# Joining two partial sums at the end of a decode kernel: fp32 identity products in PSUM, or a move to SBUF and one VectorE add

**Chip, cores, metric.** One core of one Trainium2 chip (trn2). The time is the device time of the kernel in microseconds (us); the kernel before took 367.31 us (median of 3 runs, 366.95 to 367.37). "Faster" or "slower" means a difference of more than 2%.

## The reference, cut to what matters

The output is a gated mix of two branches for 8 batch rows and 576 columns:

```python
a = softmax(q k^T * Dh**-0.5) v @ wo      # 32 heads, a window of 2048 keys, wo: (4096, 576)
b = gelu(layernorm(x) @ w1 + b1) @ w2 + b2  # w2: (4608, 576)
return g * a + (1 - g) * b
```

The kernel folds g and 1 - g into the operands, so that all products with `wo`, with `w2` and with the bias row add up in one accumulator of 8 x 576 fp32 numbers. Only the end of this accumulation is changed.

## The kernel before

The accumulator lies in one PSUM bank. The 576 columns are split into two halves of `JN` = 288 (`NJ` = 2). Each half has two copies, so that four products can run side by side in four column tiles of TensorE (in the trace before, four matmuls start within 0.01 us at 355.07): the first column-tile pair holds the halves at partitions 0 and 32, the second pair holds the same halves at partitions 64 and 96. Groups with `split=2` alternate between the pairs; groups with `split=1` use the first pair alone.

```python
class AccGroup:
    def __init__(self, name, mms, deps, cost, after=(), prio=0, split=2):
        ...
        def fn(e):
            for i, (lhsT, rhs) in enumerate(grp.mms):
                for j in range(NJ):
                    c = 64 * (i % split) + 32 * j
                    ins = e.matmul(ps[c:c + 8, BK_ACC, 0:JN], lhsT, rhs[:, JN * j:JN * j + JN], start=False, stop=True,
                                   skip_group_check=True, tile_position=(0, c))
```

The last chunk of `w2` (9 rows of 576 per partition) comes in three transfers of 4, 4 and 1 rows and goes to the first pair alone. While its first piece is multiplied, ScalarE moves the second pair's sum to SBUF; two fp32 products with an identity (the join) then add it to the first pair; the other pieces follow; at the end VectorE and ScalarE each copy one half to SBUF as bf16.

```python
cuts = [0, 4, 8, 9] if ci == FC - 1 else [0, FJ]
for n, (j0, j1) in enumerate(zip(cuts, cuts[1:])):
    ...                                    # one transfer and one AccGroup for rows j0..j1
    if ci == FC - 1 and n == 0:
        odd = [g_.op for g_ in acc_groups if g_.split == 2]
        o_ac = add("act", lambda e: e.activation(out=accs[64:128, :], in_=ps[64:128, BK_ACC, 0:JN], func=ACTF.Copy), ...)   # L807

        def join_fn(e):
            for j in range(NJ):
                c = 64 + 32 * j
                ins = e.matmul(ps[32 * j:32 * j + 8, BK_ACC, 0:JN], i32[c:c + 32, 0:8], accs[c:c + 32, :], start=False, stop=True,
                               skip_group_check=True, tile_position=(c, 32 * j))                                         # L813
        o_m2.append(add("pe", join_fn, deps=[o_ac], name="join", cost=0.7, after=o_m2[-1:]))
...
for j, (eng, ev) in enumerate((("sp", "dve"), ("act", "act"))):
    ...   # VectorE copies half 0 (L841), ScalarE half 1 (L842); then one output transfer each
```

Of the kernel before, what the change touches and what calls it, by code (L numbers as in the profile page):

```python
# [8 lines left out]
ACTF = mybir.ActivationFunctionType  # L9
ALU = mybir.AluOpType  # L10
# [28 lines left out]
class _Plan:  # L39
# [10 lines left out]
    def add(self, eng, fn, deps=(), name=None, cost=0.1, after=(), prio=0):  # L50
        op = _Op(eng, fn, deps, name, cost, after=after, prio=prio)
        op.idx = len(self.all)
        self.all.append(op)
        return op

    def dma(self, eng, fn, semkey, nbytes, deps=(), name=None, after=(), prio=0):
        op = _Op(eng, fn, deps, name, self.DMA_ISSUE, after=after, is_dma=True, dma_sem=semkey, nbytes=nbytes, prio=prio)
        op.idx = len(self.all)
        self.all.append(op)
        return op  # L60
# [121 lines left out]
def build_kernel(nc, A_x, A_k_cache, A_v_cache, A_wq, A_wo, B_x, B_w1, B_b1, B_w2, B_b2, gate_w, out):  # L182
# [10 lines left out]
    NG = Hkv // HG  # L193
# [6 lines left out]
    NJ = 2  # L200
    WO_CH = 8
    JN = D // NJ
    BIG = 1.0e9
    x2 = A_x.rearrange("b s d -> (b s) d")
    out2 = out.rearrange("b s d -> (b s) d")

    with ExitStack() as es:
# [74 lines left out]
        def view(name, parts=128):  # L282
            o, n, dt = R[name]
            a = arena[0:parts, o // 2: o // 2 + (n * (2 if dt == BF else 4)) // 2]
            if dt == F32:
                a = a.bitcast(F32)
            return a
# [5 lines left out]
        i32 = view("i32")  # L293
# [24 lines left out]
        out_sb = view("out_sb")  # L318
        accs = view("accs")
# [10 lines left out]
        def slot(s):  # L330
            return RAW[:, s * SE:(s + 1) * SE]
# [12 lines left out]
        ps = es.enter_context(nc.psum_tensor("ps", [128, 8, 512], F32))  # L344
# [5 lines left out]
        BK_ACC = 7  # L350
# [7 lines left out]
        add, dma = P.add, P.dma  # L358
# [38 lines left out]
        for s in range(2):  # L397
            o_xz.append(add("dve", (lambda s=s: lambda e: e.tensor_copy(xz[:, s, :].rearrange("p (k z) -> p k z", z=2)[:, :, s], x_sb[:, 512:576]))(),  # L398
                            deps=dx + [o_xz0], name="xz%d" % s, cost=0.12))
# [12 lines left out]
        for s in range(2):  # L412
            o_yz.append(add("dve", (lambda s=s: lambda e: e.tensor_copy(yz[:, s, :].rearrange("p (k z) -> p k z", z=2)[:, :, s], y_bf[:, 512:576]))(),
                            deps=[o_y, o_yz0], name="yz%d" % s, cost=0.12))
# [30 lines left out]
        def b1ev_fn(e):  # L445
# [5 lines left out]
                   deps=[o_dga, o_dgb, o_onesf], name="g_pe", cost=0.4, after=[o_yTp])  # L451
# [9 lines left out]
                    deps=[o_i20, o_ident], name="i2_%d" % q, cost=0.15, prio=-1) for q in range(4)]  # L461
        for q in range(4):
            o_i32.append(add("dve", (lambda q=q: lambda e: e.tensor_copy(i32[32 * q:32 * q + 32, :], ident[32 * q:32 * q + 32, 32 * q:32 * q + 32]))(),
                             deps=[o_ident, o_obl], name="i32_%d" % q, cost=0.15, prio=-1))
# [77 lines left out]
        acc_groups = []  # L542
# [32 lines left out]
        last_dma = [d_w1r]  # L575
# [4 lines left out]
        exp_done, pm_done, pt_done, pv_last = {}, {}, {}, {}  # L580
# [7 lines left out]
        def take_slot():  # L588
            n = n_slot[0]
            n_slot[0] += 1  # L590
            return 4 + n % 5
# [188 lines left out]
                        ds.append(d)  # L780
                AccGroup("proj%d" % c, mms, place_done[c] + ds, cost=1.1)

        o_m2 = []

        def bias(i):
            d = dma("sp", lambda e: e.dma_start(b2_sb, B_b2.partition_broadcast(8)), "b2", 65536, name="d_b2", after=last_dma[-1:])
# [3 lines left out]
        def m2_chunk(ci):  # L790
            s = take_slot()
            dst = slot(s)[:, 0:FJ * D]
            src = B_w2[FCW * ci:FCW * ci + FCW, :].rearrange("(p j) n -> p (j n)", j=FJ)
            cuts = [0, 4, 8, 9] if ci == FC - 1 else [0, FJ]
            ops = []
            for n, (j0, j1) in enumerate(zip(cuts, cuts[1:])):
                def w2_fn(e, j0=j0, j1=j1):
                    return e.dma_start(dst[:, j0 * D:j1 * D], src[:, j0 * D:j1 * D])
                d = dma("sp", w2_fn,
                        ("t%d" % n) if ci == FC - 1 else ("s%d" % s), 128 * (j1 - j0) * D * 2, deps=slot_free[s] if n == 0 else [], name="d_w2_%d_%d" % (ci, n), after=last_dma[-1:])  # L800
                last_dma.append(d)
                mms = [(hT[:, FJ * ci + j, :], dst[:, j * D:(j + 1) * D]) for j in range(j0, j1)]
                ops.append(AccGroup("m2_%d_%d" % (ci, n), mms, [o_hT, d], cost=0.16 * (j1 - j0), after=o_m2[-1:], split=1 if ci == FC - 1 else 2).op)
                o_m2.append(ops[-1])
                if ci == FC - 1 and n == 0:
                    odd = [g_.op for g_ in acc_groups if g_.split == 2]
                    o_ac = add("act", lambda e: e.activation(out=accs[64:128, :], in_=ps[64:128, BK_ACC, 0:JN], func=ACTF.Copy), deps=odd + pt_done[NG - 1], name="acc_ev", cost=0.5, prio=9)  # L807

                    def join_fn(e):
                        ins = None  # L810
                        for j in range(NJ):
                            c = 64 + 32 * j
                            ins = e.matmul(ps[32 * j:32 * j + 8, BK_ACC, 0:JN], i32[c:c + 32, 0:8], accs[c:c + 32, :], start=False, stop=True,  # L813
                                           skip_group_check=True, tile_position=(c, 32 * j))
                        return ins
                    o_m2.append(add("pe", join_fn, deps=[o_ac], name="join", cost=0.7, after=o_m2[-1:]))
                    ops.append(o_m2[-1])
            slot_free[s] = ops

        pv_hist = []  # L820
# [1 line left out]
        for kind, i in stream:  # L822
            if kind == "B":
                project()
            {"K": k_unit, "V": v_unit, "W": wo_chunk, "M": m2_chunk, "B": bias}[kind](i)
            while True:
                if waiting and (waiting[0] < 2 or waiting[0] - 2 in pv_last):
                    softmax(waiting[0])
                    spread(waiting.pop(0))
                elif v_here and v_here[0][0] // 4 in pt_done:  # L830
                    v_compute(*v_here.pop(0))
                else:
                    break

        acc_ops = [g_.op for g_ in acc_groups] + o_m2[-4:]
        fin = []
        for j, (eng, ev) in enumerate((("sp", "dve"), ("act", "act"))):
            def ev_fn(e, j=j, ev=ev):
                dst, src = out_sb[32 * j:32 * j + 8, :], ps[32 * j:32 * j + 8, BK_ACC, 0:JN]
                if ev == "dve":  # L840
                    return e.tensor_copy(dst, src)  # L841
                return e.activation(out=dst, in_=src, func=ACTF.Copy)  # L842
            o_fin = add(ev, ev_fn, deps=acc_ops, name="fin%d" % j, cost=0.4, prio=9)
            fin.append(dma(eng, (lambda j=j: lambda e: e.dma_start(out2[:, JN * j:JN * j + JN], out_sb[32 * j:32 * j + 8, :]))(), "out" if j == 0 else "outb", 8 * JN * 2, deps=[o_fin], name="d_out%d" % j, after=last_dma[-1:]))
        add("sp", lambda e: None, deps=fin, name="final_wait", cost=0.05)

        P.schedule()
# [16 lines left out]
def bass_gated_mix__sliding_block_cached__mixer_channel_mlp__decode_kernel(  # L864
    nc: bass.Bass,
    A_x: bass.AP,
    A_k_cache: bass.AP,
    A_v_cache: bass.AP,
    A_wq: bass.AP,
    A_wo: bass.AP,  # L870
    B_x: bass.AP,
    B_w1: bass.AP,
    B_b1: bass.AP,
    B_w2: bass.AP,
    B_b2: bass.AP,
    gate_w: bass.AP,
    out: bass.AP,
):
    build_kernel(nc, A_x, A_k_cache, A_v_cache, A_wq, A_wo, B_x, B_w1, B_b1, B_w2, B_b2, gate_w, out)
# [28 lines left out]
```

## Time and profile before

| | kernel before |
|---|---|
| time, median of 3 | 367.31 us |
| span of the profiled run | 365.8 us |
| busy: TensorE / VectorE / ScalarE | 66% / 62% / 6% |
| bytes read from HBM, mean rate | 154.31 MB, 422 GB/s |
| second piece of the last w2 chunk landed | 361.91 us |
| first of the ten matmuls behind the join | 362.84 us |
| from that landing to the end of the span | 3.89 us |

The transfer engines are full until the last slice, so only the few microseconds after the last transfers can move. I therefore read every trace by the last two rows: the time from the landing of the second piece to the end of the span does not depend on how late the 154 MB stream happens to end. The landing is the issue plus its time to landing. The lines of the profile stand in the prediction. In them PE is TensorE, PEld its weight loads, DVE VectorE, ACT ScalarE, POOL GpSimd and SP SyncE; SPq and ACTq issue transfers; L555 is line 555 of the kernel. The granted clock is the share of its full speed that TensorE was given, 1.00 or 0.50; I call the latter half clock. In before, each step between the two values comes 3.41 us, or a whole multiple of that, after the step before it (the last four are at 349.75, 353.17, 356.58 and 363.41); hence the stretches of 3.41 us below.

### The profile page before, as it was taken

The numbers are of one execution on the slowest core, as the hardware profiler recorded it, in microseconds if no ns is written. First come the engines' busy times: TensorE is split into PE (matmuls) and PEld (weight loads), VectorE is DVE, ScalarE is ACT, GpSimd is POOL, SyncE is SP. The second block draws the span as 40 slices with busy tenths as digits, with TensorE's granted clock in tenths as the row PEclk, the third lists the DMA queues.
The fourth block names the chain that finished last, engine by engine and source line by source line (L and its number), as shares of the span: only waits on it lengthen the run. The fifth ranks groups of instructions, "written<-read, shape, count | busy, mean of one in ns | idle before, by whom it ended". The sixth has DMA issues, their size and how long they took to land.

```text
span 365.8 us, 3987 instructions
## 1 busy us (share of the span) xinstructions
PE 241.1 (66%) x1683; PEld 114.5 (31%) x1683; DVE 226.3 (62%) x340; ACT 22.7 (6%) x54; POOL 17.4 (5%) x80
## 2 busy tenths in 40 slices
PE   0269684847598749365849294829948398396676
PEld 0259331312253314122514132304414133143332
DVE  4700986576999090869963453699590839975212
ACT  1010000000010000001100000001000000010000
POOL 4021000001000000010000000000000000000000
PEclk9999999689699959696987769787969588768986
DMA  9999999999999999999999999999999999999994
GB/s 393 440 415 421 423 435 443 417 456 401 457 408 447 416 439 437 423 455 407 459 403 457 405 453 408 449 416 446 417 441 423 441 409 442 423 430 432 427 420 170
DMA packets 9546, 154.58 MB, mean 423 GB/s; under 512 B 1036, under 2 KB 1204, under 8 KB 2744
## 3 DMA queue, kind: packets, MB, share of 16 engines
q1 hardware_dynamic: 9472, 154.29, 98.5%
q8 instruction: 13, 0.21, 0.2%
q10 hardware_dynamic: 56, 0.03, 0.0%
q14 instruction: 5, 0.04, 0.0%
HBM read 154.31 MB, written 0.01 MB: 422 GB/s over the span
## 4 chain that ended last, share of the span: by engine, by line
DMA 60%; DVE 25%; PE 12%; issue 2%; SPq 0%; ACT 0%; DVEq 0%
DMA arena<-in_A_k_cache_dram 54%; DVE arena L666 18%; DMA arena<-in_A_v_cache_dram 6%; PE ps L678 6%; PE ps L711 4%; DVE arena L639 3%; PE ps L555 1%; DVE arena L597 1%; DVE arena L761 1%; DVE arena L631 1%; DVE arena L600 0%; DVE arena L606 0%; PE ps L728 0%; PE ps L813 0%; PE ps L612 0%
## 5 line engine op out<-in xcount | busy, mean ns | idle before, releaser
L666 DVE STREAM_TRANSPOSE arena<-arena 128x4096 f32<-128x4096 f32 x32 | 140.7, 4424 | 88.3 <-DMA arena<-in_A_k_cache_dram 87.0
L678 PE MATMUL ps<-arena 128*32 128x512 bf16 x512 | 141.7, 440 | 62.1 <-DVE arena L666 62.1
L678 PEld LDWEIGHTS ps<-arena 128*32 128x32 bf16 x512 | 52.3, 106 | 144.3 <-DVE arena L666 67.2
L711 PE MATMUL ps<-arena 128*32 128x512 bf16 x512 | 60.7, 448 | 24.6 <-DVE arena L602 18.8
L711 PEld LDWEIGHTS ps<-arena 128*32 128x32 bf16 x512 | 24.5, 108 | 51.1 <-issue 31.4
L639 DVE STREAM_TRANSPOSE arena<-arena 128x512 bf16<-128x512 bf16 x32 | 30.8, 1021 | 0.0
L728 PE MATMUL ps<-arena 128*128 128x16 f32 x128 | 17.0, 264 | 5.8 <-ACT arena L722 3.9
L761 DVE COPY arena<-arena 32x4 bf16<-32x4 bf16 (+1 forms) x80 | 12.9, 161 | 11.3 <-POOL arena L749 9.2
L722 ACT ACTIVATE arena<-ps 128x512 f32<-128x512 f32 x16 | 9.6, 597 | 156.6 <-PE ps L711 156.6
L728 PEld LDWEIGHTS ps<-arena 128*128 128x128 f32 x128 | 15.5, 191 | 11.7 <-ACT arena L722 9.6
L749 POOL TENSOR_TENSOR arena<-arena 128x8 bf16<-128x8 f32 x30 | 5.8, 229 | 232.4 <-ACT arena L738 206.9
L510 PE MATMUL ps<-arena 128*128 128x8 bf16 x144 | 10.9, 201 | 2.8 <-DMA arena<-in_B_w_dram 2.8
L510 PEld LDWEIGHTS ps<-arena 128*128 128x128 bf16 x144 | 10.8, 168 | 3.3 <-DMA arena<-in_B_w_dram 3.3
L555 PE MATMUL ps<-arena 128*8 128x288 bf16 (+1 forms) x140 | 10.2, 369 | 2.4 <-DVE arena L761 2.2
L608 ACT ACTIVATE arena<-ps,arena 128x512 bf16<-128x512 f32 x8 | 5.5, 687 | 100.2 <-DVE arena L606 100.2
L597 DVE TENSOR_REDUCE arena<-ps 128x1 f32<-128x512 f32 x8 | 5.5, 691 | 8.8 <-PE ps L678 8.7
L659 POOL TENSOR_TENSOR arena<-arena 128x32 bf16<-128x32 bf16 x32 | 6.4, 239 | 83.7 <-PE ps L678 74.6
L612 PE MATMUL ps<-arena 128*128 128x32 f32 x16 | 3.6, 306 | 8.6 <-DVE arena L611 8.6
L631 DVE TENSOR_SCALAR arena<-arena 128x512 bf16<-128x512 bf16 x32 | 9.0, 323 | 0.0
L425 PE MATMUL ps<-arena 8*128 8x8 bf16 x8 | 0.6, 172 | 10.7 <-DVE arena L398 6.8
L512 PE MATMUL ps<-arena 128*128 128x8 bf16 x36 | 7.2, 201 | 0.0
L555 PEld LDWEIGHTS ps<-arena 128*8 128x8 bf16 (+1 forms) x140 | 4.4, 100 | 8.3 <-DVE arena L761 3.4
(87 smaller groups left out, 79.5 us busy)
## 6 DMA issues: line engine op xcount, KB each, us to landing
arena<-in_A_k_cache_dram SPq DMA_DIRECT2D x16, 4096.0 KB, 25.1
arena<-in_A_v_cache_dram SPq DMA_DIRECT2D x32, 2048.0 KB, 24.3
arena<-in_B_w_dram SPq DMA_DIRECT2D x1, 4608.0 KB, 23.8
arena<-in_A_wo_dram SPq DMA_DIRECT2D x4, 1152.0 KB, 10.0
arena<-in_A_wq_dram SPq DMA_DIRECT2D x1, 4096.0 KB, 13.1
arena<-in_B_w_dram SPq DMA_DIRECT2D x3, 1296.0 KB, 18.0
arena<-in_B_w_dram SPq DMA_DIRECT2D x3, 576.0 KB, 14.6
arena<-in_A_wq_dram SPq DMA_DIRECT2D x1, 512.0 KB, 3.4
```

What stands on the lines that cost most here:

```text
L510: ins = e.matmul(out_, lhsT, yT[:, kt, :], start=(kt == 0), stop=False)
L512: ins = e.matmul(out_, lhsT, yT[:, 4 + c // 2, :], start=False, stop=True)
L555: ins = e.matmul(ps[c:c + 8, BK_ACC, 0:JN], lhsT, rhs[:, JN * j:JN * j + JN], start=False, stop=True, skip_group_check=True, tile_position ...
L597: mx = add("dve", lambda e: e.tensor_reduce(out=k(MX), in_=ps[:, bank, :], axis=AXL.X, op=ALU.max), deps=[qk_done[g]], name="mx%d" % g, co ...
L631: return e.tensor_scalar(out=dst, in0=view("Pd").rearrange("p (s n) -> p s n", s=2), scalar1=amask[:, a:a + 1], scalar2=None, op0=ALU.mult)
L639: return e.transpose(dst, src)
L666: tr = add("dve", (lambda h=h, kb=kb: lambda e: e.transpose(bass.AP(arena_f, offset=foffs("KT") + kb * SE // 2, ap=[[AST // 2, 128], [4, 1 ...
L678: mm = e.matmul(ps[32 * c:32 * c + 32, 2 * (G % 2) + nb, :], qb[:, G % 2, n, 2 * h + ee, :], rhs, start=(h == 0 and t == 0), stop=(h == 1 ...
L711: mm = e.matmul(ps[c:c + 32, bk, :], PT[:, g % 2, 512 * q + 32 * t:512 * q + 32 * t + 32], slot(s)[:, 512 * t:512 * t + 512], start=(t < 2 ...
L722: u_ev[item] = add("act", lambda e: e.activation(out=EV[:, item % 2, :], in_=ps[:, bk, :].rearrange("p (r d j) -> p r j d", r=4, j=4), fun ...
L728: mm = e.matmul(ps[:, BK_S, OC + 16 * (item % 2):OC + 16 * (item % 2) + 16], EV[:, item % 2, 128 * r:128 * r + 128], i2[:, r, :, :].rearra ...
L761: return [add("dve", (lambda j=j, q=q: lambda e: e.tensor_copy(oT[32 * q:32 * q + 32, ch, j, bs], oN[32 * j:32 * j + 32, q, ch, bs]))(), d ...
```

## The change

Its intent: take the join off TensorE and let VectorE add the two sums while it converts to bf16, which it has to do anyway.

```diff
-    o_ac = add("act", ... activation(out=accs[64:128, :], in_=ps[64:128, BK_ACC, 0:JN], func=ACTF.Copy) ...)
-    def join_fn(e): ...                        # two fp32 identity products
-    o_m2.append(add("pe", join_fn, deps=[o_ac], name="join", cost=0.7, after=o_m2[-1:]))
-    ops.append(o_m2[-1])
+    o_ac.append(add("act", ... activation(out=accs[0:40, :], in_=ps[64:104, BK_ACC, 0:JN], func=ACTF.Copy) ...))
...
-    for j, (eng, ev) in enumerate((("sp", "dve"), ("act", "act"))): ...    # two copies, one on each engine
+    o_fin = add("dve", lambda e: e.tensor_tensor(out=out_sb[0:40, :], in0=ps[0:40, BK_ACC, 0:JN], in1=accs[0:40, :], op=ALU.add),
+                deps=acc_ops + o_ac, name="fin", cost=0.4, prio=9)
```

More of the change, by code (lines that the diff above doesn't have):

```diff
@@ L781, in project @@
                 AccGroup("proj%d" % c, mms, place_done[c] + ds, cost=1.1)
-        o_m2 = []
+        o_m2, o_ac = [], []
         def bias(i):
@@ L806, in m2_chunk @@
                     odd = [g_.op for g_ in acc_groups if g_.split == 2]
-                    o_ac = add("act", lambda e: e.activation(out=accs[64:128, :], in_=ps[64:128, BK_ACC, 0:JN], func=ACTF.Copy), deps=odd + pt_done[NG - 1], name="acc_ev", cost=0.5, prio=9)
-                    def join_fn(e):
-                        ins = None
-                        for j in range(NJ):
-                            c = 64 + 32 * j
-                            ins = e.matmul(ps[32 * j:32 * j + 8, BK_ACC, 0:JN], i32[c:c + 32, 0:8], accs[c:c + 32, :], start=False, stop=True,
-                                           skip_group_check=True, tile_position=(c, 32 * j))
-                        return ins
-                    o_m2.append(add("pe", join_fn, deps=[o_ac], name="join", cost=0.7, after=o_m2[-1:]))
-                    ops.append(o_m2[-1])
+                    o_ac.append(add("act", lambda e: e.activation(out=accs[0:40, :], in_=ps[64:104, BK_ACC, 0:JN], func=ACTF.Copy), deps=odd + pt_done[NG - 1], name="acc_ev", cost=0.5, prio=9))
             slot_free[s] = ops
@@ L833, in build_kernel @@
                     break
-        acc_ops = [g_.op for g_ in acc_groups] + o_m2[-4:]
-        fin = []
-        for j, (eng, ev) in enumerate((("sp", "dve"), ("act", "act"))):
-            def ev_fn(e, j=j, ev=ev):
-                dst, src = out_sb[32 * j:32 * j + 8, :], ps[32 * j:32 * j + 8, BK_ACC, 0:JN]
-                if ev == "dve":
-                    return e.tensor_copy(dst, src)
-                return e.activation(out=dst, in_=src, func=ACTF.Copy)
-            o_fin = add(ev, ev_fn, deps=acc_ops, name="fin%d" % j, cost=0.4, prio=9)
-            fin.append(dma(eng, (lambda j=j: lambda e: e.dma_start(out2[:, JN * j:JN * j + JN], out_sb[32 * j:32 * j + 8, :]))(), "out" if j == 0 else "outb", 8 * JN * 2, deps=[o_fin], name="d_out%d" % j, after=last_dma[-1:]))
+        acc_ops = [g_.op for g_ in acc_groups]
+        o_fin = add("dve", lambda e: e.tensor_tensor(out=out_sb[0:40, :], in0=ps[0:40, BK_ACC, 0:JN], in1=accs[0:40, :], op=ALU.add), deps=acc_ops + o_ac, name="fin", cost=0.4, prio=9)
+        fin = [dma(eng, (lambda j=j: lambda e: e.dma_start(out2[:, JN * j:JN * j + JN], out_sb[32 * j:32 * j + 8, :]))(), "out" if j == 0 else "outb", 8 * JN * 2, deps=[o_fin], name="d_out%d" % j, after=last_dma[-1:])
+               for j, eng in enumerate(("sp", "act"))]
         add("sp", lambda e: None, deps=fin, name="final_wait", cost=0.05)
```

## The prediction

> **What bounds the kernel now.** I began with the busy line and the slices of the page, to see which resource is full for most of the run.
>
> ```profile
> PE 241.1 (66%) x1683; PEld 114.5 (31%) x1683; DVE 226.3 (62%) x340; ACT 22.7 (6%) x54; POOL 17.4 (5%) x80
> ...
> PEclk9999999689699959696987769787969588768986
> DMA  9999999999999999999999999999999999999994
> ...
> HBM read 154.31 MB, written 0.01 MB: 422 GB/s over the span
> ```
>
> The DMA engines are full in 39 of 40 slices, and the row falls to 4 only in the last one (a slice is 365.8 / 40 = 9.1 us). No compute engine passes 66%. So the kernel streams 154 MB at its transfer rate for about 357 us, and then has a short tail of its own. A change that touches no transfer can only act in that tail. The changed code stands wholly there: it comes after the last quarter of w2 has begun to land. So the second view was the timeline of the last six microseconds (start, duration, engine, line, what, count, and in brackets the idle time before and what ended it).
>
> ```profile
> 358.57 3.28 PE L555 MATMUL ps<-arena 128*8 128x288 bf16 x42 [1.58 <-DVE arena L761]
> 360.56 0.74 PEld L555 LDWEIGHTS ps<-arena 128*8 128x8 bf16 x8 [0.22 <-DMA arena<-in_B_w_dram]
> 360.94 0.41 ACT L807 ACTIVATE arena<-ps 64x288 f32<-64x288 f32 x1 [6.91 <-PE ps L555]
> 361.78 1.13 PE L813 MATMUL ps<-arena 32*8 32x288 f32 x4
> 362.84 1.04 PE L555 MATMUL ps<-arena 128*8 128x288 bf16 x10
> 363.92 0.40 ACT L842 ACTIVATE arena<-ps 8x288 bf16<-8x288 f32 x1 [2.58 <-PE ps L555]
> 363.92 0.45 DVE L841 CAST arena<-ps 8x288 bf16<-8x288 f32 x1 [5.41 <-PE ps L555]
> 364.36 0.30 ACTq L844 DMA_DIRECT2D out_dram<-arena  x1
> 364.40 0.32 SPq L844 DMA_DIRECT2D out_dram<-arena  x1
> ```
>
> Read downwards: 42 accumulating matmuls (the last projection quarter 16, w2 chunk 2 18, first piece of chunk 3 8); ScalarE moves the second pair's sum to SBUF beside the 8 matmuls of that piece; the join (L813: two fp32 matmuls, recorded as four); the last 10 accumulating matmuls; two copies side by side, of which VectorE's is the longer (0.45 against 0.40); two output transfers, the SP one issued last. From its issue at 364.40 to the end of the span are 1.4 us.
>
> The chain of waits agrees that the join is on the path, and says how much of it is visible:
>
> ```profile
> 358.57 3.28 PE ps L555 x21
> 361.85 1.06 PE ps L813 x4
> 362.91 0.99 PE ps L555 x10
> 363.90 0.02 issue
> 363.92 0.45 DVE arena L841
> ```
>
> A tempting gain would be this 1.06. But the 10 matmuls behind the join wait for transfers too. The transfers of the last chunk were issued at 346.96, 347.33 and 347.81, and the DMA issues of those stretches give 13.5, 14.6 and 14.5 us to landing: they land at about 360.5, 361.91 and 362.27. The piece that follows the join could not have begun before 361.91 without the join either.
>
> The last view is the clock: busy time per stretch, in the order PE, PEld, DVE, ACT, POOL, then the granted clock, DMA share and GB/s.
>
> ```profile
> 353.17:356.58 3.41, 2.72 (x50) 1.83 (x48) 1.21 (x8) 0.60 (x1) 0.00 (x0) 1.00 1.02 431
> 356.58:360.00 3.42, 1.84 (x38) 0.81 (x32) 1.62 (x11) 0.00 (x0) 0.00 (x0) 0.50 0.92 376
> 360.00:363.41 3.41, 3.41 (x32) 1.16 (x26) 0.00 (x0) 0.41 (x1) 0.00 (x0) 0.50 0.22 81
> 363.41:365.80 2.39, 0.47 (x8) 0.10 (x4) 0.45 (x1) 0.40 (x1) 0.00 (x0) 1.00 0.02 4
> ```
>
> The join and all before it since 356.58 ran at half clock. That decides what the join costs.
>
> [...] the second pair of join records starts 0.44 us after the first (361.783 and 362.225), where a bf16 pair of the same 288 columns takes 0.24 (360.689, 360.929, 361.169, 361.409), and each join matmul has two such records, about 0.9 us of streaming against 0.24. [...] the PSUM plus SBUF fp32 add of 128x288 at L519 took 419 ns, the fp32 to bf16 multiply of the same shape at L531 459 ns, and the cast to be replaced 445 ns.
>
> **The change part by part.**
>
> *Removed: the join.* Two fp32 matmuls on TensorE. The 8 matmuls before it stream until 361.41 + 0.24 = 361.65; then the first piece behind it may start once landed, at 361.91 plus 0.04 (the first piece landed at 360.51 and its weight load began at 360.56), so at 361.95 in place of 362.84. Gain at the start of the 10 matmuls: 0.89. Of the 1.06 in the chain the transfer takes back the rest.
>
> *Moved: the clock step.* Before, the 10 matmuls straddled the step to full clock at 363.41. Starting 0.89 earlier they run wholly at half clock: pairs at 0, 0.20, 0.44, 0.68 and 0.92 (first distance as at 362.84 and 363.04, then 0.24), and the last takes 0.44: 1.36 in place of 1.04. Loss: 0.32. They end at 361.95 + 1.36 = 363.31 in place of 363.88. The third piece, landed at 362.27, is not waited for, as its pair starts at 362.87.
>
> *Added: the VectorE add* over 40 partitions in place of the cast over 8. Its time goes with the 288 elements per partition, not with partitions; from the three rows above I estimate 0.45 to 0.46 us against 0.445. Loss 0.01. It also waits for ScalarE's copy, which ended at 361.35, two microseconds before it is needed: nothing.
>
> *ScalarE's move* goes from 64 to 40 partitions and from the same to lower partitions; still 0.41 us, off the path. *ScalarE's final copy* goes; it was the shorter of two parallel ones: nothing. Both output transfers now wait for VectorE. The SP one did already and set the end; the ACT one is issued with it, 1.23 us behind in landing against 1.39. Nothing.
>
> The instruction order shows no other difference: the earlier 355 us are the same on every engine.
>
> Sum: 0.89 - 0.32 - 0.01 = 0.56 us less, with the clock phase of this trace.
>
> **The rivals.** *The clock is at full rate in the tail.* Then the last 8 matmuls end near 361.1, the join (half of 1.06, so about 0.55) is over before 361.91, and the whole of it lies under the transfer: gain 0, and 0.01 lost. Against it as the usual case: a warm tail would have made the kernel before end more than 1 us earlier, and its three times span 0.42 us. Between these lies a clock step that falls inside the join: about 0.3 to 0.5. I weigh them to a mean gain near 0.45.
> *The whole 1.06 comes back.* For it speaks only the chain; the landing at 361.91 speaks against it. It would give 366.2.
> *The add is slow* (PSUM and SBUF read together, 40 partitions, a second wait): L519 with the same operands in 419 ns speaks against it. Even twice the time would only turn the gain into about 0.1.
> *Run noise covers it.* The three runs before lie at 366.95, 367.31 and 367.37, the profiled one at 367.08. Their mean is 367.18, a little below the median, so the spread is as large as the gain.
>
> **Range and chances.** 367.18 less 0.45 is 366.73; from the median it would be 366.86; I say 366.8, which is 0.14% under the median. The half-width of 0.5 is the spread of the runs before plus the difference between the rivals: 366.3 to 367.3. Two per cent would be 7.3 us, more than the whole tail after the last transfer (365.8 - 362.3 = 3.5 us); only an upset of the transfer stream, which nothing here touches, could do it. So faster 0.01, within 2% 0.98, slower 0.01.
>
> **What would show it.** In the changed profile the first of the last ten matmuls should start within 0.1 us of the landing of the second w2 piece, with no fp32 matmul ahead; they should end about 1.36 us later at half clock or about 0.75 (an estimate: half the distances) at full clock; the add should take 0.42 to 0.48; the end should follow the output issue by about 1.4. It would be wrong if the matmuls still waited past the landing, if the add took over 0.6, or if the tail before the join ran at another clock, in which case the gain shrinks towards zero.

That the clock phase moves from run to run, on which the first rival rests, was then an assumption; the table of traces below shows it (the step listed last comes at 350.72 in join_bf16 and at 363.41 in before). That a VectorE time goes with the elements per partition rests on the times of this kernel alone: in the trace before, the cast 8x288 took 445 ns, and fp32 tensor_tensors of 128x288 and 8x576 in SBUF took 419 ns (L525) and 746 ns (L406).

## The result, and the profile after

| | before | after |
|---|---|---|
| median of 6 runs, us | 367.13 (366.24 to 367.46) | 366.84 (366.79 to 366.99) |
| ratio, 95% interval | | 0.9995 [0.9982, 1.0008] |
| second piece landed, in the trace | 361.91 | 362.31 |
| from that landing to the end of the span | 3.89 | 3.41 |

A ratio compares the mean times of the two kernels, so it is not quite the ratio of the medians. The time falls within 0.04 us of the predicted 366.8.

The timeline of the last microseconds of the changed kernel, with the columns of the prediction's second view:

```profile
359.45 2.50 PE L555 MATMUL ps<-arena 128*8 128x288 bf16 x26 [0.77 <-DMA arena<-in_B_w_dram]
360.82 0.57 PEld L555 LDWEIGHTS ps<-arena 128*8 128x8 bf16 x8 [0.56 <-DMA arena<-in_B_w_dram]
360.86 0.41 ACT L807 ACTIVATE arena<-ps 40x288 f32<-40x288 f32 x1 [8.16 <-PE ps L555]
362.35 0.81 PEld L555 LDWEIGHTS ps<-arena 128*8 128x8 bf16 x10 [0.95 <-DMA arena<-in_B_w_dram]
362.35 1.36 PE L555 MATMUL ps<-arena 128*8 128x288 bf16 x10 [0.40 <-DMA arena<-in_B_w_dram]
363.76 0.45 DVE L826 TENSOR_TENSOR arena<-ps,arena 40x288 bf16<-40x288 f32 x1 [6.58 <-PE ps L555]
364.23 0.32 SPq L827 DMA_DIRECT2D out_dram<-arena  x1
364.24 0.30 ACTq L827 DMA_DIRECT2D out_dram<-arena  x1
```

No fp32 matmul is left in the tail. TensorE now sits idle for 0.40 us before the last ten matmuls, and what ends this is the transfer. ScalarE's move is still 0.41 us, over two microseconds ahead of the add. The chain of waits ends so (start, duration, what):

```profile
349.00 13.30 DMA arena<-in_B_w_dram
362.31 0.04 issue
362.35 1.38 PE ps L555 x10
363.73 0.02 issue
363.76 0.45 DVE arena L826
```

Where the chain before came to the ten matmuls by way of 3.28 us of accumulation and 1.06 us of join, it now comes straight from the landing. And the granted clock (the first number behind the five engines) over the same stretches as before:

```profile
360.00:363.41 3.41, 3.00 (x32) 1.01 (x24) 0.00 (x0) 0.41 (x1) 0.00 (x0) 0.50 0.28 104
363.41:365.80 2.39, 0.30 (x4) 0.00 (x0) 0.45 (x1) 0.00 (x0) 0.00 (x0) 0.50 0.02 4
```

Before, the last stretch ran at 1.00, here at 0.50: the ten matmuls take 1.36 us in place of 1.04. So the join's delay of 0.89 us behind the landing is gone, a third of a microsecond of it is paid back in clock, and the stream ended 0.40 us later in this trace, which hides most of the rest in the two spans (365.8 and 365.7).

### The profile page after: what moved, and what is told of

Its sections match the earlier page's. It is cut to its first block, busy times and chain, and to the rows that moved or that the text cites. A ratio compares the mean times of both kernels' runs of the same rounds, so it can differ in the third digit from the quotient of the medians.

```text
span 365.7 us, 3979 instructions
## 1 busy us (share of the span) xinstructions
PE 239.5 (65%) x1679; PEld 114.4 (31%) x1679; DVE 226.5 (62%) x340; ACT 22.3 (6%) x53; POOL 17.4 (5%) x80
## 4 chain that ended last, share of the span: by engine, by line
DMA 63%; DVE 26%; PE 8%; issue 1%; SPq 0%; DVEq 0%
DMA arena<-in_A_k_cache_dram 54%; DVE arena L666 19%; DMA arena<-in_A_v_cache_dram 5%; PE ps L711 4%; PE ps L678 4%; DMA arena<-in_B_w_dram 4%; DVE arena L639 3%; DVE arena L597 1%; DVE arena L761 1%; DVE arena L631 1%; DVE arena L600 0%; PE ps L555 0%; DVE arena L606 0%; DVE arena L614 0%; PE ps L612 0%
```

## The experiments

Three theories stood against each other. T: the join costs only the part of it that lies past the landing of the second piece, and that only at half clock. R1: the join's whole 1.06 us is saved, and a stream that ended late took half of it away. R2: the join was hidden anyway and the difference is noise. Eleven of the twelve runs were timed in rounds against the kernel before, in three calls, the first on one chip and the other two on another. The kernels before and after were run again among them. One caution for the third call (the lean kernels and after_third): of the ten runs of the kernel before that it lists, nine are those of the second call, and the one new run took 366.08 us. The traces of all runs but the two with other cuts, in one table (us; "delay" is the start of the first of the last ten matmuls minus the landing; a normal wait has 0.04):

| trace | second piece landed | delay | landing to end | TensorE clock in the tail |
|---|---|---|---|---|
| before | 361.91 | 0.93 | 3.89 | half, full from 363.41 |
| before_again | 361.92 | 0.85 | 3.76 | half, full from 363.21 |
| join_one_cast | 362.45 | 0.77 | 4.16 | half from 355.55 |
| join_twice | 362.08 | 1.65 | 4.93 | half from 357.65 |
| join_bf16 | 362.03 | 0.33 | 3.64 | half from 350.72 |
| after | 362.31 | 0.04 | 3.41 | half from 354.98 |
| after_again | 362.20 | 0.04 | 3.40 | half from 360.21 |
| after_third | 362.09 | TensorE never idle | 3.50 | half from 350.72 |
| before_warm | 361.95 | 0.32 | 3.03 | full from 350.99 |
| after_warm | 362.18 | TensorE never idle | 2.98 | full from 353.07 |
| before_lean | 362.89 | 0.05 | 2.74 | full from 354.19 |
| after_lean | 362.10 | 0.05 | 3.41 | full, half from 362.19 |

**after_again.** No edit; the changed kernel with five rounds.

> The changed kernel once more, with more rounds. T (the join costs only the part of it that lies past the landing of the second w2 piece, and that part only at half clock): 0.2 to 0.5 us under the kernel before in the mean; from the landing of the second w2 piece to the end of the span 3.4 us at half clock against 3.9 in the trace of before. R1 (the whole 1.06 us of the join is saved, and the transfer stream happened to end 0.4 us later in the trace of after): 0.9 to 1.1 us in the mean. R2 (the join is hidden anyway): 0.0 to 0.1 us.

Measured: ratio 0.9989 [0.9976, 1.0002], which is 0.40 us of 367.2 less; 3.40 us from landing to end. Both are what T said; R1's 0.9 to 1.1 us lies outside the interval (0.88 us less to 0.07 more). R2's value of nothing lies in it, so the times alone do not rule R2 out.

**join_twice.**

```diff
             ins = e.matmul(ps[32 * j:32 * j + 8, BK_ACC, 0:JN], i32[c:c + 32, 0:8], accs[c:c + 32, :], start=False, stop=True, ...)
+        for j in range(NJ):
+            c = 64 + 32 * j
+            ins = e.matmul(ps[32 * j:32 * j + 8, 0, 0:JN], i32[c:c + 32, 0:8], accs[c:c + 32, :], start=True, stop=True, ...)
```

> The kernel before with the two fp32 matmuls done a second time, into an unused PSUM bank. T: the first join already reaches past the landing of the second piece at half clock, so the second adds its whole streaming time of 0.9 to 1.06 us to the span where the tail is at half clock, and 0.2 to 0.5 where the tail is at full clock; mean +0.6 to +1.0 us against before. R2 (hidden): +0.0 to +0.2. R1 does not differ from T here.

Measured: ratio 1.0034 [1.0021, 1.0047], 1.25 us more, with 0.77 to 1.73 in the interval. The chain of waits:

```profile
361.78 1.06 PE ps L813 x4
362.84 0.96 PE ps L817 x4
363.80 1.32 PE ps L555 x6
```

The second join (L817) stands in the chain with its whole 0.96 us. R2's 0.0 to 0.2 lies outside the interval: join time that reaches past the landing is paid for. That the first join reached past it is not shown by this run, but by the delays of 0.93, 0.85 and 0.77 us in the table, against 0.04 for a normal wait; so R2 falls for a tail at half clock. The mean is above T's 0.6 to 1.0, though the interval reaches into it; why it is above stays open.

**join_bf16.**

```diff
-over("accs", "P", 0, JN, F32)
+over("accs", "P", 0, JN, BF)
-            ins = e.matmul(..., i32[c:c + 32, 0:8], accs[c:c + 32, :], ...)
+            ins = e.matmul(..., ident[c:c + 32, c:c + 8], accs[c:c + 32, :], ...)
```

> The kernel before with the second sum moved to SBUF as bf16 and the join done with bf16 identity products, one pass of 0.24 us in place of about 0.9. T: a join that short ends by the landing of the second piece (361.65 + 0.24 = 361.89 against 361.91 in the trace of before), so it costs nothing: time as the changed kernel within 0.1 us, landing to end of span 3.3 to 3.5 us at half clock. R1 (every part of the join lies on the path): about 0.25 us above the changed kernel, landing to end 3.6 to 3.7. R2: as before.

Measured: ratio 0.9988 [0.9973, 1.0002], the same as the changed kernel in the same rounds (0.9989), and the output was still correct. But in the trace the short join cost something, which T had not expected:

```profile
358.82 3.28 PE ps L555 x22
362.11 0.33 PE ps L813 x2
362.43 1.31 PE ps L555 x10
```

The short join, recorded as two matmuls where the fp32 join has four, is in the chain with 0.33 us, and landing to end is 3.64, R1's value and not T's. Here the clock had been at half since 350.72, the value products ended late, and TensorE had not paused since 358.82. The last pair of matmuls ahead of the join started at 361.66, against 361.41 in the trace of before, and the join began at 362.04, just after the landing at 362.03. Without the join the ten matmuls would have been ready one pair distance (0.24) later, at 361.90, and would have started 0.04 after the landing, at 362.07; they started at 362.36. So I estimate that 0.29 us of the join reached past the landing. With the output path about 0.06 shorter than in the changed kernel (1.42 from the SP issue to the end, against 1.48) this makes 0.23, which is 3.64 - 3.41. T's rule holds, then; what failed is its assumption that TensorE gets to the join as early as in the trace of before.

**join_one_cast.** The other half of the change alone: the join kept, one VectorE instruction at the end.

```diff
-    for j, (eng, ev) in enumerate((("sp", "dve"), ("act", "act"))): ...
+    o_fin = add("dve", lambda e: e.tensor_copy(out_sb[0:40, :], ps[0:40, BK_ACC, 0:JN]), deps=acc_ops, ...)
```

> The kernel before with its join kept, but with one VectorE cast of 40 partitions in place of the two copies on VectorE and ScalarE: the other half of the change alone. T and R1: VectorE's copy set the end already, so no change, within 0.1 us of before; the cast of 40 partitions takes 0.44 to 0.46 us. A rival R3 (the two copies disturb one another in one PSUM bank, and the single final instruction is what gains): 0.3 us or more under before.

Measured: ratio 1.0007 [0.9993, 1.0020], no gain seen (at most 0.26 us by the interval), so R3's 0.3 or more falls. Its timeline gives the join's cost with the tail wholly at half clock:

```profile
362.16 1.13 PE L813 MATMUL ps<-arena 32*8 32x288 f32 x4
363.22 1.36 PE L555 MATMUL ps<-arena 128*8 128x288 bf16 x10
364.63 0.45 DVE L836 CAST arena<-ps 40x288 bf16<-40x288 f32 x1 [7.17 <-PE ps L555]
```

The ten matmuls take 1.36 us as in the changed kernel, so the two traces compare without any term for the clock: 4.16 - 3.41 = 0.75 us from landing to end, against delays of 0.77 and 0.04. That is the join's price at half clock where the landing is the gate. The cast over 40 partitions takes as long (0.45) as the one over 8 did.

**before_again.** No edit, one look.

> The kernel before once more, for a second trace with its own clock phase. T: from the landing of the second w2 piece to the end of the span 4.1 to 4.2 us if the tail is at half clock throughout, 3.9 as in the first trace if the step to full clock falls in the last ten matmuls, and down to 2.8 to 3.1 if the join and the ten matmuls run at full clock. R1: always about 1.0 above the 3.4 of the changed kernel at half clock. R2: 3.4.

Measured: 366.96 us (one run), landing to end 3.76, with the step to full clock at 363.21, in the ten matmuls: T's second case, 0.14 under the value named. R1's value would have been 4.4, R2's 3.4.

**before_warm and after_warm.** Filler products with zero weights, into an unused PSUM bank, after the bias (3), behind w2 chunk 0 (12), behind the last projection quarter (10) and behind w2 chunk 2 (3). They were to hold the clock at full.

```diff
+    def fill_fn(e):
+        for _ in range(n):
+            ins = e.matmul(ps[:, 0, 0:320], zeros_bf, ones_bf, start=True, stop=True, skip_group_check=True)
```

> The kernel before with 28 filler matmuls (zero weights, an unused PSUM bank) in TensorE's idle gaps after the last value product, so that the tail runs at full clock; the last group behind the join is not delayed by them. T: the join is then over before the second w2 piece has landed and costs nothing: landing to end 2.8 to 2.9 us, and the time within 0.1 us of the filled changed kernel; 0.7 to 1.1 us under before. R1: 0.4 to 0.6 us above the filled changed kernel. If the fillers do not raise the clock, or hold up the accumulations, the run says nothing on this.

> The changed kernel with the same fillers. T: the last ten matmuls take about 0.75 us in place of 1.36, so landing to end 2.8 us in place of 3.4; 0.5 to 0.6 us under the changed kernel, 0.9 to 1.1 under before, and equal to the filled kernel before within 0.1. R1: 0.4 to 0.6 under the filled kernel before.

Measured: before_warm 0.9973 [0.9960, 0.9987], after_warm 0.9973 [0.9961, 0.9986], both about 1.0 us under before. The kernels with and without the join came out equal, as T says and R1 does not (0.4 to 0.6 apart). But by the condition named beforehand this pair says nothing on the rivals: landing to end was 3.03 and 2.98, not the 2.8 expected, because the fillers held up the accumulations in both, and in before_warm the ten matmuls still started 0.32 us after the landing, behind the join. Of the clock the two traces show that it was full from before the first filler (350.99 and 353.07 against 352.79 and 353.56) through the last ten matmuls (0.78 us in before_warm), where the eight traces without fillers in the table are at half clock ahead of the ten. So I thinned the fillers.

**before_lean and after_lean.** The same with 3, 10, 4 and 0 fillers.

> The filled kernel before with 17 fillers in place of 28 (3 behind the bias, 10 behind w2 chunk 0, 4 behind the last projection quarter, none later): in the first filled pair the fillers themselves held up the accumulations (the first piece of chunk 3 landed at 360.57 and began at 361.10, so the join still reached 0.3 us past the landing). T: at full clock the join now ends before the second piece lands; landing to end 2.8 to 2.9 us; time equal to the lean changed kernel within 0.1 us. R1: 0.4 to 0.6 above it. If too few fillers leave the tail at half clock, landing to end is 3.7 to 4.2 as in the traces of before.

> The changed kernel with the same 17 fillers. T: landing to end 2.8 us at full clock, equal to the lean kernel before within 0.1 us; 0.4 to 0.7 us under the unfilled changed kernel of the same rounds. At half clock 3.4 as without fillers.

Measured: before_lean 0.9966 [0.9952, 0.9979], after_lean 0.9980 [0.9966, 0.9993]. The timeline of before_lean shows the join wholly covered:

```profile
360.80 1.41 PE L555 MATMUL ps<-arena 128*8 128x288 bf16 x26
362.13 0.65 PE L823 MATMUL ps<-arena 32*8 32x288 f32 x4
362.94 0.78 PE L555 MATMUL ps<-arena 128*8 128x288 bf16 x10 [0.15 <-DMA arena<-in_B_w_dram]
```

At full clock the join takes 0.65 us, is over at 362.78, and TensorE then waits another 0.15 us for the transfer that landed at 362.89. The fp32 join costs nothing there. R1 is refuted in this phase. That after_lean came out about 0.5 us slower than before_lean by the ratios (0.4 by the plain means), and not equal, none of the theories had expected. Its trace shows how that can be:

```profile
362.15 1.36 PE L555 MATMUL ps<-arena 128*8 128x288 bf16 x10 [0.72 <-DMA arena<-in_B_w_dram]
```

The clock fell to half at 362.19, just as the ten matmuls began, and they took 1.36 us again. One trace cannot say whether it falls more often there because TensorE, without the join, stands idle before them, or by chance of phase; this stays open. In the 3.41 us before the fall, TensorE was busy for 1.48; the join would have added about 0.65. But a busy time near that decides nothing by itself: the clock stayed full after a stretch with 1.51 (join_twice, 347.41 to 350.82) and fell after one with 2.72 (before, 353.17 to 356.58); and in join_bf16 it stayed at half after 354.13 to 357.54, in which TensorE was busy throughout. What sets the clock is not shown. The two intervals overlap.

**after_cuts.**

```diff
-cuts = [0, 4, 8, 9] if ci == FC - 1 else [0, FJ]
+cuts = [0, 3, 6, 8, 9] if ci == FC - 1 else [0, FJ]
```

> The changed kernel with the last w2 chunk cut into pieces of 3, 3, 2 and 1 rows in place of 4, 4 and 1. T: without the join the end is set by the matmuls that are left when the piece before the last lands: three pairs in place of five, 0.44 + 0.44 us in place of 1.36, so the time 0.4 to 0.5 us under the changed kernel and 0.8 to 0.9 under before. A rival R4 (the end is set by the output transfer and the sequence of final instructions alone): no change against the changed kernel.

Measured: 0.9976 [0.9962, 0.9989], so 0.88 us under before; but the unaltered changed kernel on the same chip (after_third, below) has 0.9981, only 0.2 us away and inside the interval. The gain expected of the cuts is not shown; this is also what the rival R4 said. In the trace TensorE ran from 359.17 to 363.67 without a pause at half clock, so smaller last pieces had nothing to shorten.

**after_third.** No edit.

> The changed kernel unaltered, beside the filled ones in the same rounds. T: 0.3 to 0.5 us under before in the mean, 0.4 to 0.7 us above the lean filled changed kernel; its own trace 3.4 us from landing to end at half clock.

Measured: 0.9981 [0.9967, 0.9994], 0.7 us less than before, more than T's 0.3 to 0.5, and with R1's 0.9 to 1.1 inside the interval. But the runs of before are nearly all of the earlier call, and the one new one (366.08) lies under all four of after_third (366.51 to 366.95), so this is weak evidence for any size. Nor was the lean changed kernel 0.4 to 0.7 us faster, as T had it: its ratio is 0.9980. In the trace of after_lean full clock was lost just as the ten matmuls began. The trace of after_third is of the same phase as that of join_bf16, half clock since 350.72:

```profile
359.08 4.49 PE L555 MATMUL ps<-arena 128*8 128x288 bf16 x52 [0.93 <-DVE arena L761]
363.61 0.45 DVE L826 TENSOR_TENSOR arena<-ps,arena 40x288 bf16<-40x288 f32 x1 [4.58 <-PE ps L555]
```

All 52 last matmuls run in one piece. The second piece landed at 362.09, just in time for the ten matmuls, which started at 362.16, one pair distance (0.24) behind the pair before; TensorE at half clock is the bound, by a few hundredths of a us.

**after_cuts_lean.** Both together: fillers 3, 10, 4, 0 and cuts 3, 3, 2, 1.

> The changed kernel with the 17 fillers and the last w2 chunk cut 3, 3, 2, 1. In its half-clock trace the cut kernel was held up by TensorE from 359.17 to 363.67 without a pause, so the smaller pieces could not help there. T: at full clock TensorE keeps up, three pairs are left at the landing of the piece before the last: about 0.24 us under the filled changed kernel with cuts of 4, 4, 1; 0.9 to 1.3 under before. If the cuts do nothing at full clock either, equal to it.

Measured: 0.9962 [0.9950, 0.9975], 1.4 us under before, with all five runs between 366.03 and 366.13. The after_third runs of the same chip lie between 366.51 and 366.95. The trace:

```profile
361.47 0.53 PE L555 MATMUL ps<-arena 128*8 128x288 bf16 x6 [0.55 <-DMA arena<-in_B_w_dram]
362.16 0.65 PE L555 MATMUL ps<-arena 128*8 128x288 bf16 x6 [0.15 <-DMA arena<-in_B_w_dram]
362.86 0.45 DVE L836 TENSOR_TENSOR arena<-ps,arena 40x288 bf16<-40x288 f32 x1 [5.04 <-PE ps L555]
```

TensorE waits for each piece, and 0.65 us of matmuls are left behind the last wait that the line shows. That is to be compared with the ten matmuls at full clock, 0.78 in before_lean, and not with their 1.36 at half clock. This version beats both kernels, though still by far less than 2%. Against the lean kernel without the cuts (0.9980) it is better by 0.7 us, more than the 0.24 expected; most of that is the clock, which stayed full here until 364.87 and fell at 362.19 there. The cuts alone are not shown to be worth anything: from the landing of the piece before the last to the end are 2.70 us here and 2.74 in before_lean, which has the join and the old cuts, and whose ratio of 0.9966 lies inside this interval. What both share is the fillers.

## Why the prediction was right, point by point

- **The tail alone can move, and the landing takes most of the join's 1.06 us back.** Right in kind. The changed kernel's ten matmuls start 0.04 us after the landing in two traces (0.07 in after_third), as said. Before, they started 0.93 and 0.85 us after it.
- **The clock step.** The ten matmuls were put at 1.36 us at half clock and took 1.36. The predicted distance of 0.89 - 0.32 - 0.01 = 0.56 us is 3.89 - 3.41 = 0.48 in the traces; the rest is the path behind the add, where the end came 1.48 us after the SP output issue in place of 1.40. The prediction had put the output transfers at nothing, but this stretch is 1.48 to 1.50 us in all eight traces with one VectorE instruction at the end and 1.40 to 1.42 in all six with two copies, so about 0.07 us of the gain is lost there. Why is not shown.
- **The add.** Estimated at 0.45 to 0.46 us, measured 0.45 (450 ns over 40 partitions with bf16 output, where the cast over 8 took 445 and the PSUM add over 128 with fp32 output, L519, 419). One cast of 40 partitions in place of two copies (join_one_cast) brought no gain, as the prediction said of that part; the longer output path came with it (1.50 us).
- **The full-clock rival.** Right, and now shown: with the join in place but the tail at full clock, the join was over before the landing and the end came 2.74 us after it (3.89 in before). The join itself took 0.65 us there and not the 0.55 named.
- **What was wrong: the whole 1.06 was ruled out.** The prediction let the landing at 361.91 speak against it. That holds where TensorE reaches the join well ahead of that landing. In the phase of join_bf16 and after_third TensorE had not paused since about 359, and in join_bf16 the join began only as the piece landed. An fp32 join begun there at 362.04 would have held the ten matmuls until 363.10, 1.03 us past the 362.07 at which they could start. This is an estimate, as no kernel with the fp32 join was traced in that phase.
- **What was wrong: the phase was judged steady.** From three times within 0.42 us the prediction took a warm tail to be rare. The kernel before ran between 366.08 and 368.07 us over all rounds, the changed one between 366.51 and 367.05. The before spread fits a join that costs anything from nothing to its whole length by clock phase; that it is the reason is not shown. The stream has a spread of its own: the second piece landed between 361.91 and 362.89 in the traces of the table.
- **The mean gain.** Weighed at 0.45 us; the three comparisons give 0.18 (0.9995), 0.40 (0.9989) and 0.70 (0.9981), each computed from about 367.2 us. Only the third interval excludes no gain, and it rests on runs of another call. So what is shown is the mechanism, in the traces; a gain in the mean time is likely but not shown. That the time came within 0.04 us of 366.8 is luck: the runs of before in that table span 1.22 us, and their median came out 0.18 under the one from which the prediction had started. The range itself was a safe one for a change that can only act in the last few microseconds.

## What to carry to other kernels

A busy span in the chain of waits is worth only what of it reaches past the next thing waited for (here 0.75 us for a join of 1.06 us at half clock, nothing for one of 0.65 at full clock); look up when the transfer behind it lands before counting the span as a gain. When TensorE's clock in a short tail is half in one run and full in another (here 1.36 or 0.78 us for the same ten matmuls), work out the saving for each phase, and measure from the landing to the end of the span, not span against span. In the fastest kernels here TensorE was kept busy ahead of the tail (before_lean 0.9966, after_cuts_lean 0.9962), with the join or without it.
